# A chunked scan with a gated feed-forward layer: six steps in another order, last rows copied by whole banks, and one output matmul for both parts of a weight

## The chip, the cores and the metric

The kernel runs on 1 core of one Trainium2 chip. The metric is the time of one execution on the device in microseconds (us), and a kernel's time is the median of its runs. "Profile" and "trace" mean the records that the hardware profiler made of one execution. The engines are named as the profile names them: PE is TensorE (PEld its weight loads), DVE VectorE, ACT ScalarE, POOL GpSimd, SP SyncE.

## The reference, cut to what matters

Four batches of eight heads and 768 positions go through a scan with decay, in chunks. The result, 3072 rows of 256, goes through a gated layer with 1536 inner columns.

```python
for c in range(S // chunk):                    # the scan, per batch and head
    L = exp(cum[:, None] - cum[None, :]) * causal
    y_intra = ((C_c @ B_c.T) * L) @ x_c
    y_inter = (C_c @ state) * exp(cum)
    y[c] = y_intra + y_inter
    state = exp(sum(la)) * state + (B_c * decay_from_j).T @ x_c
x = y, as rows of 256
gate = 1 / (1 + exp(-(x @ w_gate)))            # 3072 x 1536
out  = (gate * (x @ w_val)) @ w_out            # 3072 x 256
```

## The kernel before, in words

**Tiles.** The 768 positions are six chunks of 128, and a chunk has the rows of all four batches, 512 columns. `w_gate` and `w_val` are twelve blocks each of 128 inner columns. Where precision needs it, a matrix is kept as a high and a low part, and a product is three matmuls: high by high, high by low, low by high.

**Stages.** First come chunk 0 and the preparation of the weights. Then, for each chunk, twelve pairs of gate and value products (`gate`, `value`), 128x512 each: ACT takes the sigmoid of the gate's bank, DVE multiplies the value's bank by it (L1206), ACT or DVE casts the result to the high part of h (L1210), POOL or DVE subtracts for the low part (L1212). The scan of later chunks runs between them: small matmuls in blocks (`block`), and on DVE the decays' scan (L575), six small steps a pair of batches for the state (`after`: mask L677, update L755 twice, mask, update twice), the weighing of a block (`weights`, L778) and a transposition (`turn`, L840). `proj` multiplies h by `w_out`.

**The last two chunks** (T2 = 4 and T1 = 5) go through gate and value together, as a 2x2 product by seven instead of eight blocks: for each of twelve groups (`group`, even ones gate, odd ones value) seven products of three matmuls each on combined inputs (L1369). `corner` puts four results together from three banks: ACT copies a bank to a tile (L1402), DVE adds another bank to it (L1404), then comes the sigmoid (L1407) for a gate group, or a multiplication with the gate's result (L1411) for a value group; the corner "12" is one bank alone (L1391, L1395). `h_parts` makes the two parts of h: a cast on ACT (L1421), a subtraction on DVE or POOL (L1423). `out_of` multiplies them by `w_out` and adds up in four banks (L1445): each step takes two of the four batches, and for each batch three matmuls of 256 columns: high h by both weight parts, low h by the high part. The names 11, 22, 12, 21 give inner block and chunk; 11 and 21 go to chunk T1. `stored_rows` copies one batch at a time, 256 columns, from a bank to a tile (L1459) and stores it, 128 KB (L1461): eight copies and eight stores.

**Order.** Nothing is scheduled at run time. The text `ORDER` names each step with its engine; a step issues its instructions in that place of its engine's queue, and the engines work their queues in order. Three banks of `ps_mm` are handed round among gate products, value products and `proj`; a product's step waits until the bank from three tiles before was read. In the groups each bank has its own turn: a value group's corner 12 must be read by DVE before the next gate group's third product can start in that bank.

Of the kernel before, what the change touches and what calls it, by code (L numbers as in the profile page):

```python
# [65 lines left out]
pool.decays3_0 dve.after2_0 pe.value1_2 sp.a3_2 act.gate1_2 dve.after2_0 dve.after2_0 pool.part14  # L66
dve.weights2_2 sp.a3_3 pe.gate1_3 dve.value1_2 pool.before2_2 act.part15 sp.b3_2 dve.after2_0 act.value1_2
pe.value1_3 sp.x3_0 dve.after2_0 act.gate1_3 sp.p3_0 pool.value1_2 dve.weights2_2 pe.gate1_4 dve.value1_3
sp.a4_0 pool.part15 act.value1_3 pe.value1_4 sp.a4_1 dve.turn3_0 act.gate1_4 act.part16 pe.gate1_5
pool.value1_3 sp.t3_2 act.turn3_0 dve.value1_4 dve.value1_4 pool.part16 pe.value1_5 act.gate1_5 pool.value1_4  # L70
act.part17 pe.block2 dve.value1_5 pool.part17 act.value1_5 pool.value1_5 pe.gate1_6 dve.result2_0 act.inner2_2
sp.x3_2 dve.decays3_1 act.result2_0 pe.value1_6 act.gate1_6 pool.result2_0 dve.after2_2 dve.weights3_0
pe.gate1_7 pool.decays3_1 dve.result2_0 sp.b4_0 pool.before3_0 dve.value1_6 act.result2_0 sp.a4_2
pool.result2_0 pe.value1_7 dve.weights3_0 act.value1_6 dve.after2_2 act.gate1_7 sp.a4_3 pool.value1_6
pe.gate1_8 dve.value1_7 act.value1_7 dve.after2_2 pe.value1_8 dve.after2_2 act.gate1_8 pool.value1_7
pe.gate1_9 dve.value1_8 dve.after2_2 act.value1_8 dve.after2_2 pe.value1_9 act.gate1_9 pool.value1_8 sp.p3_2
pe.gate1_10 dve.value1_9 dve.turn3_2 act.value1_9 pe.value1_10 act.gate1_10 pool.value1_9 sp.t4_0 act.turn3_2
pe.gate1_11 dve.value1_10 dve.decays3_2 act.value1_10 pe.value1_11 act.gate1_11 pool.value1_10 pe.block3
dve.value1_11 pool.decays3_2 act.value1_11 dve.decays3_3 pe.proj1_0 pool.value1_11 dve.result2_2 act.inner3_0
# [10 lines left out]
dve.weights4_2 act.gate2_2 sp.t5_0 pool.result3_2 dve.weights4_2 pool.decays5_0 pe.gate2_3 dve.result3_2  # L90
pool.decays5_1 dve.value2_2 act.result3_2 pool.result3_2 pe.value2_3 act.value2_2 dve.after4_0 act.gate2_3
pool.value2_2 pe.gate2_4 dve.value2_3 sp.p4_2 dve.after4_0 act.value2_3 dve.after4_0 pe.value2_4 dve.after4_0
sp.x5_0 act.gate2_4 pool.value2_3 pe.gate2_5 dve.value2_4 pool.before4_2 act.value2_4 pe.value2_5 dve.after4_0
# [33 lines left out]
pe.group2 act.part0_12 dve.part0_21 pe.group2 dve.corner2_11 pool.part0_12 pe.group2 act.corner2_11 pe.out0_11  # L127
act.corner2_21 pe.group2 dve.corner2_21 pe.out0_22 act.corner2_21 dve.corner2_22 pe.out0_22 act.corner2_22
pe.group2 pe.group3 act.corner2_12 dve.s8 pe.group3 act.corner3_11 dve.s8 pe.out0_12 act.corner3_22 pe.group3
act.s8 pe.group3 dve.corner3_11 pool.s8 pe.group3 act.corner3_21 pe.out0_12 dve.corner3_11 pe.group3  # L130
dve.corner3_21 act.part1_11 pe.out0_21 dve.corner3_22 pool.corner3_21 pe.out0_21 pe.group3 dve.corner3_22
act.part1_21 pe.group4 dve.part1_11 act.part1_22 pe.group4 dve.part1_22 act.corner4_11 pe.out1_11
dve.corner3_12 pool.part1_21 act.corner4_22 pe.group4 act.part1_12 dve.part1_12 pe.group4 pe.group4
dve.corner4_11 pool.s9 act.corner4_21 pe.out1_11 act.corner4_11 dve.corner4_21 pe.group4 dve.s9 act.corner4_21
pe.out1_22 dve.corner4_22 act.s9 pe.out1_22 act.corner4_22 dve.s9 pe.group4 pe.group5 act.corner4_12 dve.s10
pe.group5 act.corner5_11 dve.s10 pe.out1_12 act.corner5_22 pe.group5 act.s10 pe.group5 dve.corner5_11 pool.s10
pe.group5 act.corner5_21 pe.out1_12 dve.corner5_11 pe.group5 dve.corner5_21 act.part2_11 pe.out1_21
dve.corner5_22 pool.corner5_21 pe.out1_21 pe.group5 dve.corner5_22 act.part2_21 pe.group6 dve.part2_11
act.part2_22 pe.group6 dve.part2_22 act.corner6_11 pe.out2_11 dve.corner5_12 pool.part2_21 act.corner6_22
pe.group6 act.part2_12 dve.part2_12 pe.group6 pe.group6 dve.corner6_11 pool.s11 act.corner6_21 pe.out2_11  # L140
act.corner6_11 dve.corner6_21 pe.group6 dve.s11 act.corner6_21 pe.out2_22 dve.corner6_22 act.s11 pe.out2_22
act.corner6_22 dve.s11 pe.group6 pe.group7 act.corner6_12 pe.group7 act.corner7_11 pe.out2_12 act.corner7_22
pe.group7 pe.group7 dve.corner7_11 pe.group7 act.corner7_21 dve.corner7_11 pe.out2_12 dve.corner7_21
act.part3_11 pe.group7 dve.corner7_21 pe.out2_21 dve.corner7_22 pool.part3_11 act.part3_21 pe.out2_21
pe.group7 dve.corner7_22 pe.group8 dve.corner7_12 pool.part3_21 act.part3_22 pe.group8 act.corner8_11
pe.out3_11 dve.part3_22 act.part3_12 pe.group8 act.corner8_22 dve.part3_12 pe.group8 dve.corner8_11 pe.group8
act.corner8_11 pe.out3_11 act.corner8_21 pe.group8 dve.corner8_21 pe.out3_22 act.corner8_21 dve.corner8_22
pe.out3_22 act.corner8_22 pe.group8 pe.group9 act.corner8_12 pe.group9 act.corner9_11 pe.out3_12
act.corner9_22 pe.group9 pe.group9 dve.corner9_11 pe.group9 act.corner9_21 dve.corner9_11 pe.out3_12
# [50 lines left out]
def tile_ssd_then_gated_ffn(  # L200
# [11 lines left out]
    nc = tc.nc  # L212
# [1250 lines left out]
    def joined_tasks(t):  # L1463
# [14 lines left out]
        for k in (T2, T1):  # L1478
            for at in range(2):
                task(t + 110.0 + (k == T1), f"rows{k}_{at}", stored_rows(k, at))  # L1480
# [374 lines left out]
```

## Time and profile before

| | |
|---|---|
| runs of the kernel | 355.91, 357.05, 356.99 us |
| median | 356.99 us |
| the profiled execution | 356.6 us |
| its span, first to last instruction | 354.7 us |
| PE busy | 345.0 us, 97% of the span, 3328 matmuls |
| PE weight loads | 277.1 us, 78% |
| DVE busy | 230.5 us, 65% |
| ACT busy | 175.1 us, 49% |
| POOL busy | 170.3 us, 48% |
| moved by DMA | 27.43 MB, mean 77 GB/s |
| mean granted TensorE clock | 0.998 of full speed |

A timeline row has the start and the duration in us, the engine, the line, the operation, its tiles as out<-in, the shape and the count of instructions merged in it; in brackets stands how long the engine was idle just before and what ended that. Rows of matmuls overlap, since a matmul's duration has its way through the array in it: starts tell the pace. PE busy is no measure of how well PE is used.

### The profile page before, as it was taken

The numbers are of one execution on the slowest core, as the hardware profiler recorded it, in microseconds if no ns is written. First come the engines' busy times: TensorE is split into PE (matmuls) and PEld (weight loads), VectorE is DVE, ScalarE is ACT, GpSimd is POOL, SyncE is SP. The second block draws the span as 40 slices with busy tenths as digits, with TensorE's granted clock in tenths as the row PEclk, the third lists the DMA queues.
The fourth block names the chain that finished last, engine by engine and source line by source line (L and its number), as shares of the span: only waits on it lengthen the run. The fifth ranks groups of instructions, "written<-read, shape, count | busy, mean of one in ns | idle before, by whom it ended". The sixth has DMA issues, their size and how long they took to land.

```text
span 354.7 us, 8271 instructions
## 1 busy us (share of the span) xinstructions
PE 345.0 (97%) x3328; PEld 277.1 (78%) x3328; DVE 230.5 (65%) x405; ACT 175.1 (49%) x330; POOL 170.3 (48%) x179
## 2 busy tenths in 40 slices
PE   8989999999999999999999999999999999999995
PEld 3568477787778888888888788888888888888884
DVE  6778668787697677684653246358765778574462
ACT  2575874425946541244551235543546565654533
POOL 6435676646769664235646746864101615032100
PEclk9999999999999999999999999999999999999999
DMA  7999884335655635634300011000002000000003
GB/s 160 221 262 216 248 258 135 110 79 95 134 130 126 129 70 113 105 77 90 63 16 4 2 37 24 0 0 2 1 0 61 1 0 2 0 0 2 0 2 118
DMA packets 87467, 27.43 MB, mean 77 GB/s; under 512 B 75718, under 2 KB 80262, under 8 KB 87430
## 3 DMA queue, kind: packets, MB, share of 16 engines
q1 hardware_dynamic: 82838, 26.13, 31.3%
q10 hardware_dynamic: 4592, 0.79, 1.2%
q8 instruction: 26, 0.43, 0.5%
q14 instruction: 11, 0.09, 0.1%
HBM read 23.46 MB, written 3.44 MB: 76 GB/s over the span
## 4 chain that ended last, share of the span: by engine, by line
PE 64%; DVE 4%; ACT 1%; POOL 1%; issue 1%; ACTq 0%; DVEq 0%; POOLq 0%
PE po L1506 14%; PE pg L1245 13%; PE pv L1245 12%; PE acc L1445 6%; PE gva L1369 6%; PE gvb L1369 5%; PE gvd L1369 4%; PE banks L785 1%; DVE c L1404 1%; DVE h L1423 1%; PE banks L769 1%; ACT h L1421 1%; PE banks L815 1%; POOL c L1411 1%; DVE c L1411 1%
## 5 line engine op out<-in xcount | busy, mean ns | idle before, releaser
L1212 POOL TENSOR_TENSOR h<-g,h 128x512 fp32r<-128x512 f32 x35 | 47.4, 1356 | 36.5 <-ACT h L1210 35.2
L1245 PE MATMUL pg<-xh,w 128*128 128x512 f32 x168 | 59.4, 394 | 0.9 <-DVE g L1206 0.9
L1245 PE MATMUL pv<-xh,w 128*128 128x512 f32 x168 | 58.9, 391 | 0.1
L1506 PE MATMUL po<-h,w 128*128 128x512 f32 x216 | 51.3, 392 | 0.0
L1206 DVE TENSOR_TENSOR g<-pv,g 128x512 f32<-128x512 f32 x36 | 24.8, 689 | 35.2 <-PE pv L1245 34.7
L1506 PEld LDWEIGHTS po<-h,w 128*128 128x128 f32 x216 | 40.2, 188 | 8.6
L1445 PEld LDWEIGHTS acc<-w,h 128*128 128x128 f32 x288 | 38.8, 190 | 3.2 <-DVE h L1423 0.4
L1445 PE MATMUL acc<-w,h 128*128 128x256 f32 x288 | 39.9, 283 | 0.2 <-DVE h L1423 0.2
L1210 ACT CAST h<-g 128x512 fp32r<-128x512 f32 x34 | 21.1, 621 | 36.5 <-DVE g L1206 36.4
L1245 PEld LDWEIGHTS pg<-xh,w 128*128 128x128 f32 x168 | 31.5, 188 | 9.1 <-DVE g L1206 1.3
L1245 PEld LDWEIGHTS pv<-xh,w 128*128 128x128 f32 x168 | 31.5, 188 | 7.2 <-POOL w L497 0.5
L1245 PE MATMUL pg<-xl,w 128*128 128x512 f32 x84 | 32.7, 390 | 0.0
L1245 PE MATMUL pv<-xl,w 128*128 128x512 f32 x84 | 32.7, 389 | 0.0
L1185 ACT ACTIVATE g<-pg 128x512 f32<-128x512 f32 x44 | 26.3, 599 | 12.5 <-PE pg L1245 12.3
L497 POOL TENSOR_TENSOR w<-wr,w 128x512 fp32r<-128x512 f32 x18 | 25.8, 1437 | 7.5 <-ACT w L495 7.1
L575 DVE TENSOR_TENSOR_SCAN ab<-ab,delta 128x512 f32<-128x512 f32 x20 | 27.1, 1374 | 2.3 <-DMA ab<-a_z 2.3
L1423 POOL TENSOR_TENSOR h<-c,h 128x512 fp32r<-128x512 f32 x7 | 11.4, 1646 | 35.5 <-ACT h L1421 35.5
L478 POOL TENSOR_TENSOR wr<-wr 128x512 int32<-128x512 int32 x18 | 20.0, 1115 | 12.7 <-ACT wr L476 7.9
L1545 PE MATMUL po<-wr,h 128*128 128x256 f32 x96 | 23.4, 394 | 0.2 <-DVE h L1202 0.2
L1421 ACT CAST h<-c 128x512 fp32r<-128x512 f32 x24 | 14.7, 622 | 16.4 <-DVE c L1411 13.0
L1404 DVE TENSOR_TENSOR c<-gva,c 128x512 f32<-128x512 f32 x12 | 8.3, 691 | 20.8 <-PE gva L1369 20.8
L1545 PEld LDWEIGHTS po<-wr,h 128*128 128x128 f32 x96 | 17.6, 188 | 4.4 <-DVE h L1202 0.7
(191 smaller groups left out, 664.4 us busy)
## 6 DMA issues: line engine op xcount, KB each, us to landing
ab<-a_z SPq DMA_DIRECT2D x40, 128.0 KB
wr<-in_moe_w_gate_dram SPq DMA_DIRECT2D x6, 512.0 KB
wr<-in_moe_w_val_dram SPq DMA_DIRECT2D x6, 512.0 KB
wr<-in_moe_w_out_dram SPq DMA_DIRECT2D x6, 512.0 KB
xn<-in_x_dram SPq DMA_DIRECT2D x10, 256.0 KB
out_dram<-o SPq DMA_DIRECT2D x48, 32.0 KB
bn<-in_B_dram SPq DMA_DIRECT2D x10, 128.0 KB
out_dram<-o SPq DMA_DIRECT2D x9, 128.0 KB
```

The lines of the kernel that those rows point to most:

```text
L478: nc.gpsimd.tensor_tensor(out=lw.bitcast(I32), in0=hw.bitcast(I32), in1=lw.bitcast(I32), op=ALU.add)
L497: engines[eng].tensor_tensor(out=lo, in0=lw, in1=hi.bitcast(F32), op=ALU.subtract)
L575: nc.vector.tensor_tensor_scan(out=t.rearrange("p h l -> p (h l)"), data0=t.rearrange("p h l -> p (h l)"), data1=delta.rearrange("p h l -> ...
L1185: nc.scalar.activation(gs[k, f], pm, AF.Sigmoid)
L1206: nc.vector.tensor_tensor(out=g, in0=pm, in1=g, op=ALU.mult)
L1210: copies[eng](hh, g)
L1212: engines[eng].tensor_tensor(out=hl, in0=g, in1=hh.bitcast(F32), op=ALU.subtract)
L1245: nc.tensor.matmul(pm, w[:, part, kt, fs], xx[:, kt], start=(i == 0), stop=(i == 3 * NK - 1))
L1369: nc.tensor.matmul(out, one, two, start=m == 0 and n in (1, 7, 2), stop=m == 2, skip_group_check=True)
L1445: nc.tensor.matmul(acc[:, k * DM : (k + 1) * DM], one(js), w[:, two, :], start=first and m == k == 0, stop=final and m == 2, skip_group_ch ...
L1506: nc.tensor.matmul(acc, w[:, part], hs[k, f][:, of_h], start=f == starts[0] and i == 0, stop=f == starts[-1] + size - 1 and i == 2,)
L1545: nc.tensor.matmul(acc[:, :DM], hs[k, f][:, js], whole[NF + f // 2][:, f % 2], start=start, stop=stop, skip_group_check=True,)
```

## The change

Six places of the order move, as each engine's own queue sees them:

- DVE: value1_2 goes ahead of the third and fourth step of `after2_0` and of the first weighing of pair 2_2; value1_3 goes ahead of the second weighing.
- ACT: the copy of corner2_21 goes ahead of the sigmoid of corner2_11.
- DVE: corner3_12 goes ahead of the low part of h for 1_22, and corner5_12 ahead of that for 2_22.
- PE: the second half of out4_21 goes ahead of the last but one product of group 11.
- DVE and ACT: corner11_12 and the parts of h for 5_12 go ahead of corner11_21's multiplication and the parts for 5_21; the steps that copy the last rows are new.

In the last step the rows of chunk T2 and the first two batches of T1 are copied from a whole bank (512 columns) to one tile of 2 KB in each partition, and stored with one DMA of 256 KB. The other two batches of T1 (`at` = 1) have a bank each, a fourth bank of the pool `ps_gv` being added: high h is multiplied by both weight parts in one matmul of 512 columns into the two halves of the bank, low h by the high part into the left half. The last step of `out_of` puts all three into the left half, so the right half is complete one step before: ACT copies the right half (`last_rows`), and DVE adds the left one to it behind the last matmul.

The diff, cut: of the order's text only the moved steps with their neighbours in the engine's own queue, of the code the functions whose work changes.

```diff
-dve.after2_0 dve.after2_0 dve.after2_0 dve.after2_0 dve.weights2_2 dve.value1_2
-dve.after2_0 dve.after2_0 dve.weights2_2 dve.value1_3 dve.turn3_0
+dve.after2_0 dve.after2_0 dve.value1_2 dve.after2_0 dve.after2_0 dve.weights2_2
+dve.after2_0 dve.after2_0 dve.value1_3 dve.weights2_2 dve.turn3_0
...
-act.part0_21 act.part0_12 act.corner2_11 act.corner2_21 act.corner2_21
+act.part0_21 act.part0_12 act.corner2_21 act.corner2_11 act.corner2_21
...
-dve.part1_11 dve.part1_22 dve.corner3_12 dve.part1_12
+dve.part1_11 dve.corner3_12 dve.part1_22 dve.part1_12
...
-dve.part2_11 dve.part2_22 dve.corner5_12 dve.part2_12
+dve.part2_11 dve.corner5_12 dve.part2_22 dve.part2_12
...
-pe.out4_12 pe.group11 pe.out4_21 pe.group11 pe.out4_21 pe.group11 pe.out5_22
+pe.out4_12 pe.group11 pe.out4_21 pe.out4_21 pe.group11 pe.group11 pe.out5_22
...
-dve.part5_11 dve.part5_22 dve.corner11_21 dve.corner11_21 dve.corner11_12
-dve.part5_21 dve.part5_12 dve.rows5_0 dve.rows5_1
+dve.part5_11 dve.part5_22 dve.corner11_12 dve.corner11_21 dve.part5_12
+dve.corner11_21 dve.part5_21 dve.rows4_1 dve.rows5_2 dve.rows5_3
-act.part5_22 act.part5_21 act.part5_12 act.rows4_0 act.rows4_1 act.rows4_0
-act.rows4_1 act.rows5_0 act.rows5_0 act.rows5_0 act.rows5_1 act.rows5_1
+act.part5_22 act.part5_12 act.part5_21 act.rows5_2 act.rows5_3 act.rows4_0
+act.rows5_0 act.rows5_0 act.rows5_3
-sp.rows4_0 sp.rows4_1 sp.rows4_0 sp.rows4_1 sp.rows5_1
+sp.rows4_0 sp.rows4_1 sp.rows5_2
...
         if ("acc", block, at) not in bank:
             if (block, at) == (T1, 1):
                 bank["acc", block, at] = ps_y.tile([P, 512], F32, tag="py", name="acc")
+            elif (block, at) == (T1, 2):
+                bank["acc", block, at] = bank["pool"].tile([P, 512], F32, tag="e", name="acce")
...
             for k in range(2):
                 js = slice((2 * at + k) * P, (2 * at + k + 1) * P)
+                alone = block == T1 and at == 1
+                acc = acc_of(block, at + k if alone else at)
+                mine = acc[:, :DM] if alone else acc[:, k * DM : (k + 1) * DM]
+                if alone and not final:
+                    nc.tensor.matmul(
+                        acc, hh(js), w.rearrange("p i m -> p (i m)"), start=first, stop=False, skip_group_check=True
+                    )
+                    nc.tensor.matmul(mine, hl(js), w[:, 0, :], start=False, stop=False, skip_group_check=True)
+                    continue
                 for m, (one, two) in enumerate(((hh, 0), (hh, 1), (hl, 0))):
                     nc.tensor.matmul(
-                        acc[:, k * DM : (k + 1) * DM], one(js), w[:, two, :], start=first and m == k == 0,
-                        stop=final and m == 2, skip_group_check=True,
+                        mine, one(js), w[:, two, :], start=first and m == 0 and (k == 0 or alone), stop=final and m == 2,
+                        skip_group_check=True,
                     )
...
     def stored_rows(k, at):
...
-        for n in range(2):
-            b = 2 * at + n
-            eng = yield step(("act", "dve"), (ACT_HALF, DVE_HALF), [("o7", j, last, at)])
...
-            half = acc_of(k, at)[:, n * DM : (n + 1) * DM]
-            copies[eng](o.rearrange("p (m t) -> p t m", t=2), half.rearrange("p (t m) -> p t m", t=2))
...
+        eng = yield step(("act", "dve"), (ACT_MM, DVE_MM), [("o7", NF // 2 - 1, "21" if k == T1 else "12", at)])
+        o = wk.tile([P, 2, DM], F32, tag="m", name=f"o{k}_{at}", bufs=4)
+        copies[eng](o.rearrange(by_tk, t=2), acc_of(k, at).rearrange(by_k, k=2, t=2))
+        eng = yield step(("sp", "act"), (0.45, 0.36))
+        (nc.scalar if eng == "act" else nc.sync).dma_start(rows_of(k, 2 * at, 2), o)
+
+    def last_rows(b):
+
+        yield step("act", ACT_HALF, [("o7", NF // 2 - 1, "11", 1)], [("low", b)])
+        acc = acc_of(T1, b - 1).rearrange(by_k, k=2, t=2)
+        o = wk.tile([P, 1, DM], F32, tag="o", name=f"o{T1}_{b}", bufs=2)
+        by_t = o.rearrange(by_tk, t=2)
+        nc.scalar.copy(by_t, acc[:, 1:])
+        yield step("dve", DVE_HALF, [("o7", NF // 2 - 1, "21", 1)])
+        nc.vector.tensor_tensor(out=by_t, in0=acc[:, :1], in1=by_t, op=ALU.add)
+        eng = yield step(("sp", "act"), (0.45, 0.36))
+        (nc.scalar if eng == "act" else nc.sync).dma_start(rows_of(T1, b, 1), o)
```

## Rows read from the trace of the kernel before

**Rows 1.** The chain that ended last, from the page: its shares of the span by engine.

```profile
PE 64%; DVE 4%; ACT 1%; POOL 1%; issue 1%; ACTq 0%; DVEq 0%; POOLq 0%
```

**Rows 2.** Waits of PE from 100 us on: us in total, times, longest us.

```profile
PE pg L1245 <- DVE g L1206: 0.9, 1, 0.9
PE gvb L1369 <- DVE c L1395: 0.6, 2, 0.4
```

**Rows 3.** Timeline of PE at the step from value1_3 to gate1_4.

```profile
101.64 0.39 PE L1245 MATMUL pv<-xh,w 128*128 128x512 f32 x1
102.91 0.50 PE L1245 MATMUL pg<-xh,w 128*128 128x512 f32 x1 [0.88 <-DVE g L1206]
```

**Rows 4.** Timeline of DVE, 99 to 105 us.

```profile
99.61 1.85 DVE L755 SCALAR_TENSOR_TENSOR sm<-sq,pp,ml 128x64 f32<-128x64 f32 x2
...
102.18 0.68 DVE L1206 TENSOR_TENSOR g<-pv,g 128x512 f32<-128x512 f32 x1
102.78 0.47 DVE L755 SCALAR_TENSOR_TENSOR sn<-sm,pp,mr 128x64 f32<-128x64 f32 x2
...
104.09 0.69 DVE L1206 TENSOR_TENSOR g<-pv,g 128x512 f32<-128x512 f32 x1 [0.25 <-issue]
```

**Rows 5.** Timeline of POOL, 99 to 105 us.

```profile
101.33 0.73 POOL L857 TENSOR_TENSOR cd<-bct,pp 128x256 f32<-128x256 f32 x1
103.58 1.29 POOL L1212 TENSOR_TENSOR h<-g,h 128x512 fp32r<-128x512 f32 x1 [1.51 <-ACT h L1210]
104.84 1.56 POOL L497 TENSOR_TENSOR w<-wr,w 128x512 fp32r<-128x512 f32 x1
```

**Rows 6.** Timeline of POOL and DVE, 86.4 to 88.3 us.

```profile
86.45 1.30 POOL L497 TENSOR_TENSOR w<-wr,w 128x512 fp32r<-128x512 f32 x1 [0.35 <-ACT w L495]
86.51 1.70 DVE L607 SCALAR_TENSOR_TENSOR sn<-sm,pp,mr 128x64 f32<-128x64 f32 x2
...
87.71 0.41 POOL L585 TENSOR_TENSOR bd<-bn,ab 128x128 f32<-128x128 f32 x1
```

**Rows 7.** Timeline in the last two chunks, group 2 and then group 4.

```profile
269.19 0.87 PE L1445 MATMUL acc<-w,h 128*128 128x256 f32 x6
...
269.50 0.57 ACT L1402 COPY c<-gva 128x512 f32<-128x512 f32 x1
...
270.11 0.53 PEld L1369 LDWEIGHTS gva<-xt,s 128*128 128x128 f32 x3 [0.27 <-ACT c L1402]
...
280.31 2.38 DVE L1423 TENSOR_TENSOR h<-c,h 128x512 fp32r<-128x512 f32 x2
...
282.10 0.87 PE L1445 MATMUL acc<-w,h 128*128 128x256 f32 x6
...
283.35 0.96 PE L1369 MATMUL gvb<-x,w 128*128 128x512 f32 x3 [0.37 <-DVE c L1395]
...
284.15 0.85 PE L1369 MATMUL gva<-xt,s 128*128 128x512 f32 x3
```

**Rows 8.** The chain in order of time, 283 to 292 us: start, us on the chain, what.

```profile
285.68 0.71 PE acc L1445 x6
286.39 0.69 PE gva L1369 x3
```

**Rows 9.** Timeline of the tail, from 342 us on.

```profile
342.38 1.46 DVE L1423 TENSOR_TENSOR h<-c,h 128x512 fp32r<-128x512 f32 x2
...
345.64 1.23 ACT L1421 CAST h<-c 128x512 fp32r<-128x512 f32 x2 [2.53 <-DVE c L1411]
...
348.43 0.39 ACT L1459 COPY o<-acc 128x256 f32<-128x256 f32 x1 [1.56 <-PE acc L1445]
348.84 2.54 SPq L1461 DMA_DIRECT2D out_dram<-o  x5
```

**Rows 10.** DMA from 345 to 355 us, in 40 slices, and what was moved.

```profile
GB/s 0 0 0 0 0 0 0 0 0 0 0 0 0 0 0 0 0 0 33 344 148 78 348 185 352 344 336 348 340 328 348 332 316 17 0 0 0 0 0 0
DMA packets 1152, 1.05 MB, mean 105 GB/s; under 512 B 128, under 2 KB 1152, under 8 KB 1152
```

More of the change, by code (lines that the diff above doesn't have):

```diff
@@ L65 @@
 pool.value1_1 dve.before2_0 dve.decays3_0 act.part14 pe.gate1_2 act.inner2_0 sp.a3_1 dve.after2_0
[L66 to L79, printed above, removed]
@@ L90 @@
[L90 to L93, printed above, removed]
+pool.decays3_0 dve.after2_0 pe.value1_2 sp.a3_2 act.gate1_2 dve.value1_2 dve.after2_0 dve.after2_0 pool.part14
@@ new lines @@
+dve.weights2_2 sp.a3_3 pe.gate1_3 pool.before2_2 act.part15 sp.b3_2 dve.after2_0 act.value1_2 pe.value1_3
+sp.x3_0 dve.after2_0 act.gate1_3 sp.p3_0 pool.value1_2 dve.value1_3 dve.weights2_2 pe.gate1_4 sp.a4_0
+pool.part15 act.value1_3 pe.value1_4 sp.a4_1 dve.turn3_0 act.gate1_4 act.part16 pe.gate1_5 pool.value1_3
+sp.t3_2 act.turn3_0 dve.value1_4 dve.value1_4 pool.part16 pe.value1_5 act.gate1_5 pool.value1_4 act.part17
+pe.block2 dve.value1_5 pool.part17 act.value1_5 pool.value1_5 pe.gate1_6 dve.result2_0 act.inner2_2 sp.x3_2
@@ L131 @@
[L131 to L135, printed above, removed]
@@ L162 @@
+dve.corner11_22 pe.out4_21 pe.group11 dve.part5_11 act.part5_22 dve.part5_22 pe.group11 dve.corner11_12
+dve.corner11_21 act.part5_12 pe.out5_22 pe.out5_22 dve.part5_12 dve.corner11_21 pe.out5_11 act.part5_21
+pe.out5_11 act.rows5_2 act.rows5_3 dve.part5_21 pe.out5_12 pe.out5_12 pe.out5_21 pe.out5_21 act.rows4_0
+sp.rows4_0 dve.rows4_1 sp.rows4_1 act.rows5_0 act.rows5_0 dve.rows5_2 sp.rows5_2 dve.rows5_3 act.rows5_3
 """
@@ L1363, in group @@
                 scan_banks.close()
-                ps_gv = ctx.enter_context(tc.tile_pool(name="ps_gv", bufs=1, space=PSUM))
+                ps_gv = bank["pool"] = ctx.enter_context(tc.tile_pool(name="ps_gv", bufs=1, space=PSUM))
                 bank["gv"] = [ps_gv.tile([P, 512], F32, tag=n, name=f"gv{n}") for n in "adb"]
@@ L1477, in joined_tasks @@
                 task(t + 15.0 * j + (15.0, 18.0, 21.0, 24.0)[m], f"out{j}_{n}", out_of(j, n))
-        for k in (T2, T1):
-            for at in range(2):
-                task(t + 110.0 + (k == T1), f"rows{k}_{at}", stored_rows(k, at))
+        for k, at in ((T2, 0), (T2, 1), (T1, 0)):
+            task(t + 110.0 + (k == T1), f"rows{k}_{at}", stored_rows(k, at))
+        for b in range(2, NB):
+            task(t + 112.0, f"rows{T1}_{b}", last_rows(b))
     gs = {}
```

104 lines of the change are left out of this document (57 added, 47 removed).

## The prediction

> **What bounds the kernel now.** I read the chain that ended last first: 64% of it is TensorE [rows 1]. So a change pays where TensorE stands still, where it has less to issue, or behind its last product. The table of waits then says where it stands still after 100 us [rows 2], and the timeline gives each wait its place.
>
> The first is among the gate and value products of chunk 1. The last matmul of value1_3 starts at 101.64, gate1_4 only at 102.91 [rows 3]: 1.27 us from start to start where three such matmuls take 0.69 [rows 8], 0.23 each, so 1.04 us are lost. Gate1_4 waits for a bank that VectorE empties with the multiplication at 102.18 [rows 4].
>
> The others are in the last two chunks, where seven products make a group. There six output matmuls take 0.71 and a product 0.69 [rows 8]. Output matmuls that start at 282.10 should let the next product start at 282.81; it starts at 283.35, and the one behind it 0.80 later instead of 0.69 [rows 7]: 0.65 lost. Its twin, one pair of groups later, has what is left of the 0.6 us of idle time [rows 2], 0.2; in the first one 0.37 of idle time went with 0.65 of loss, so the twin lost about 0.2 and the same 0.28, 0.50. At 270.11 ScalarE is late: 269.19 and 0.71 make 269.90, so 0.21, and 0.11 of start-up again, 0.33 lost [rows 7].
>
> Last I read the tail [rows 9] and the slices of its DMA [rows 10], each of 0.25 us. The first store is issued at 348.84; bytes begin to move at the end of the slice that ends at 349.75, 0.89 later. The flow stalls twice (slices of 148 and 78, then of 185 GB/s), and runs from 351.0 to 353.25 without a gap at 316 to 352 GB/s. 1.05 MB at some 340 GB/s is 3.1 us. The span ends 1.4 us behind the last byte (354.7 less 353.25). So the end is set by the start of the first store and by the gaps in the flow, less by the last matmul.
>
> The profiled execution took 356.6 us: its span of 354.7 and 1.9 around it. The median of the runs is 356.99 and one had 355.91. The sum is made against 356.6.
>
> **Part 1: two value products (VectorE) ahead of steps of the state.** value1_2 now stands behind one of the two small state updates instead of both, the mask step and the weighing. The updates begin at 99.61 [rows 4], so it runs at 99.9 instead of 102.18. Gate1_4 then finds its bank free at 101.87. What is late next is value1_3: gate1_5 needs its bank twelve matmuls later, at 104.6, and ahead of it on VectorE still stand the mask step, the weighing (these end at 102.2, as before) and the second pair of state updates. That pair is the trap. ScalarE's cast follows the earlier value1_2, so GpSimd's subtraction for that tile, at 103.58 after 1.51 us of idle time, moves to 102.06, right behind the operation of 0.73 at 101.33; its next one, of 1.56, then follows without a pause [rows 5]. The updates take 0.47 at 102.78 with GpSimd idle, but 1.85 at 99.61 [rows 4]; at 86.51 a pair took 1.70, while GpSimd worked from 86.45 and again from 87.71 [rows 6]: each update waits out one GpSimd operation. So with the pair due at 102.2, the first is held to about 103.4, the second, behind the operation of 1.56, to about 104.9, and value1_3 ends at 105.6, not at 104.78. Gate1_5 starts at 105.6, where it stood at 105.76 before (102.91, twelve matmuls, 0.11). Of 1.04 I keep 0.15. The ends are 0 (the whole stop moves) and 1.04 (no hold). I take 0.15, nearest to rows 6, the same kind of pair beside a busy GpSimd. Behind value1_3 on VectorE wait a weighing and a transposition, wanted by the block of small matmuls after value1_5; they shift by 0.8, and have 2.7 us until then. The table has no other wait of TensorE until the last two chunks [rows 2], so what is won here stays won.
>
> By the Trainium skill, "SBUF — State Buffer", section "Who interferes with whom", a VectorE instruction with two SBUF inputs contends with GpSimd's reads, and one with a single SBUF input does not; rows 4 to 6 agree, and by it the pair is held. Without it the sum would be 0.9 us lower, which is the first rival.
>
> **Part 2: corner2_21's copy ahead of corner2_11's sigmoid on ScalarE.** The copy runs at 269.50 [rows 7], behind a sigmoid that it doesn't depend on. Ahead of it, it ends before 269.90, and 0.33 is won. The sigmoid comes some 0.5 later; its result is first multiplied a group later. Ends 0.2 (start-up stays) and 0.33.
>
> **Part 3: corner3_12 and corner5_12 ahead of a subtraction on VectorE.** Two subtractions took 2.38 at 280.31 [rows 7], where two take 1.46 in rows 9; corner3_12 stood behind them. Between them it starts at 281.0 and ends at 281.7; TensorE wants its bank at 282.81. It reads a bank and one tile, like the multiplication at 104.09, which took 0.69 beside GpSimd's operation from 103.58 [rows 4, 5]. The subtraction behind it was held before, and is held no longer now. Gains 0.65 and 0.50; ends half of each and the whole.
>
> **Part 4: six output matmuls ahead of a product that waits, near the end (TensorE), and the last group's corners in a new order.** This covers short stops, but the tail hangs on the first store, whose corners are VectorE's and ScalarE's to make: 0 by itself. What it could be worth is in part 6's upper end.
>
> **Part 5: h by both weight parts.** For two batches of the last chunk, in 11 of 12 steps, two matmuls of 256 columns on the same h become one of 512. A 256 takes 0.71/6 = 0.118, a 512 0.69/3 = 0.230 or a little less [rows 8]: 0.006 to 0.011 for each of 22 pairs, 0.13 to 0.24; I take 0.2, as pairs in the tail don't count. Ends 0 and 0.24. The bank that is added was another tile's before and is idle by then.
>
> By the Trainium skill, "TensorE: Matmul & The Clock Gate", section "Back-to-back issue gap", 256 columns take 262 cycles and 512 take 518; as an estimate from that page a pair would win 0.0025 us, and the sum would come out 0.15 higher.
>
> **Part 6: the stores.** Eight half copies and eight stores of 128 KB become three whole copies, four half operations, three stores of 256 KB and two of 128. From the end of the two subtractions at 343.84 [rows 9] I lay out the new order: corner11_12 and corner11_21's add (0.61 and 0.69), ScalarE's cast beside the second, a subtraction (0.69), corner11_21's multiplication (0.61): 346.45. ScalarE casts (0.62, a pair takes 1.23 in rows 9), then does two half copies that need no late matmul (0.39 alone, 0.3 each in a row), then the first whole copy, 0.57 as in rows 7: about 348.15. So the first store goes out 0.7 earlier than at 348.84. The other whole copies and the adds follow the last matmuls with stores at 348.75, 349.4, 349.6 and 350.0, each before the flow that begins at 349.05 has worked off the one before. So the gaps close, and the flow ends 3.1 us after 349.05, at 352.15 against 353.25. Gain 1.1. Ends 0.4 (the gaps alone) and 1.5 (part 4 brings the last corners 0.4 forward as well).
>
> **The sum.** 0.15 + 0.33 + 0.65 + 0.50 + 0.2 + 1.1 = 2.93: 353.7 us. I say 353.6, since part 1 has more room to win than to lose.
>
> **The rivals.** First, the second update isn't held: part 1 gives 1.04, 352.7. For it: GpSimd's operation has only 0.1 us on the update (102.06 against 102.2). Against it: rows 6. Chance 0.24. Second, the tail gives nothing: the two half copies stand ahead of the first whole copy on ScalarE, the first store is no earlier than now, and the flow starts late and has all of 1.05 MB before it: 354.7. For it: in rows 9 the first copy waits for matmuls and nothing else. Against it: the gaps in rows 10. Chance 0.14. Third, the moves don't do what they say: behind each removed wait the next dependency of the same bank comes as late, as in part 1, and under 1.07 us is left, some 356. For it: a bank is handed round between three engines. Against it: VectorE ends corner3_12 a full 1.1 us ahead of need. Chance 0.07. Fourth, slower: the holds of part 1 spread to the block after value1_5. It is due at 108.3 (105.6 and twelve matmuls); if it is late by over 4.0 us (2.93 and 1.07), the end lies above 357.7. That takes three more holds of 1.3 to 1.6 in VectorE's queue. For it: GpSimd's work there has no pause after its move. Against it: what stands behind value1_3 reads banks or one tile. Chance 0.04. The forecast has 0.51.
>
> **The numbers.** 0.3% is 1.07 us, about what a measurement here can tell from no change. Faster by more: 0.51 + 0.24 + 0.14 = 0.89; within: 0.07; slower: 0.04. The range runs from all upper ends (1.04, 0.33, 1.15, 0.24, 1.5: 352.3, less 0.2 for the spread of runs) to the second rival and the 0.4 by which the median lies above the profiled run: 352.1 to 355.1.
>
> **What would show it.** Right: no wait of 0.9 at gate1_4 but one of about 0.9 at gate1_5, with the second pair of updates at 2.5 us or more; no wait on L1395; products 0.69 apart around 270, 282 and 299; the flow of stores in slices of 330 to 350 GB/s without a gap. Wrong: no wait at either gate (first rival), a flow that starts as late behind the last group as now (second), or a stop of TensorE after the block (fourth).

## The result, and the profile after

The changed kernel took 352.18 us (median of 5 runs, 351.94 to 352.82) against 356.99 us of the kernel before: a ratio of 0.9878, interval 0.9861 to 0.9896. The forecast was 353.6 us, range 352.1 to 355.1. The profiled execution took 352.14 us with a span of 350.4, so it is compared with 356.6 and 354.7 of before: 4.3 us of span.

The waits of PE in the changed kernel, whole span (us in total, times, longest us):

```profile
PE warm L259 <- DVE table L264: 1.1, 1, 1.1
PE pg L1140 <- POOL wr L477: 0.7, 1, 0.7
PE pg L1140 <- ACT xw L1066: 0.5, 2, 0.3
PE pcb L657 <- DVE m L640: 0.2, 1, 0.2
```

None of them lies behind 60 us. Both rows of [rows 2] are gone, and so is a third of before, which [rows 2] leaves out and the forecast passed over (waits of PE, kernel before):

```profile
PE acc L1445 <- DVE h L1423: 0.2, 1, 0.2
```

**The gates of chunk 1.** PE at the steps value1_3 to gate1_4 and value1_4 to gate1_5, then DVE, POOL and SP around them, in the changed kernel:

```profile
100.94 0.39 PE L1244 MATMUL pv<-xh,w 128*128 128x512 f32 x1
101.16 0.39 PE L1244 MATMUL pg<-xh,w 128*128 128x512 f32 x1
...
103.66 0.39 PE L1244 MATMUL pv<-xh,w 128*128 128x512 f32 x1
103.88 0.39 PE L1244 MATMUL pg<-xh,w 128*128 128x512 f32 x1
```

```profile
99.14 0.68 DVE L1205 TENSOR_TENSOR g<-pv,g 128x512 f32<-128x512 f32 x1
...
101.44 0.95 DVE L754 SCALAR_TENSOR_TENSOR sn<-sm,pp,mr 128x64 f32<-128x64 f32 x2
102.32 0.68 DVE L1205 TENSOR_TENSOR g<-pv,g 128x512 f32<-128x512 f32 x1
...
101.48 0.83 POOL L856 TENSOR_TENSOR cd<-bct,pp 128x256 f32<-128x256 f32 x1 [0.84 <-DMA pp<-a_q]
102.27 1.29 POOL L1211 TENSOR_TENSOR h<-g,h 128x512 fp32r<-128x512 f32 x1
...
98.39 1.22 SPq L429 DMA_DIRECT2D pp<-a_q  x2
```

Both gates follow 0.22 us behind the matmul ahead of them, where gate1_4 stood 1.27 behind in [rows 3]. The second pair of state updates took 0.95 us, not the 2.5 or more that was forecast, because GpSimd's `cd` came late: GpSimd stood idle for 0.84 us until the load `pp` had landed, and its subtraction (102.27) started only when both updates had begun.

**The last two chunks.** PE at group 2 and at group 4, and DVE's corner3_12 (L1394):

```profile
267.38 0.39 PE L1449 MATMUL acc<-w,h 128*128 128x512 f32 x1
...
268.06 0.88 PE L1368 MATMUL gva<-xt,s 128*128 128x512 f32 x3
...
279.94 0.88 PE L1455 MATMUL acc<-w,h 128*128 128x256 f32 x6
280.65 0.86 PE L1368 MATMUL gvb<-x,w 128*128 128x512 f32 x3
281.35 0.85 PE L1368 MATMUL gva<-xt,s 128*128 128x512 f32 x3
```

```profile
278.18 0.68 DVE L1422 TENSOR_TENSOR h<-c,h 128x512 fp32r<-128x512 f32 x1
278.78 0.69 DVE L1394 TENSOR_TENSOR c<-gvb,c 128x512 f32<-128x512 f32 x1
279.38 1.18 DVE L1422 TENSOR_TENSOR h<-c,h 128x512 fp32r<-128x512 f32 x1
```

Six output matmuls at 279.94 take 0.71 and the product behind them 0.70; [rows 7] had 1.25 and 0.80 there. The step at 267.38, now four matmuls, takes 0.68 (to the product's start at 268.06), where [rows 7] had 0.92 from 269.19 to the weight load at 270.11.

**The tail.** PE from the last product in bank gva on, ScalarE's first copies and SP's first stores; then the flow, from 340 to 352 us in slices of 0.3 us:

```profile
335.26 0.85 PE L1368 MATMUL gva<-x,w 128*128 128x512 f32 x3
...
340.15 2.51 PE L1455 MATMUL acc<-w,h 128*128 128x256 f32 x18
...
343.21 2.68 PE L1455 MATMUL acc<-w,h 128*128 128x256 f32 x21
345.72 0.52 PE L1455 MATMUL acce<-w,h 128*128 128x256 f32 x3
```

```profile
343.83 0.40 ACT L1479 COPY o<-acce 128x256 f32<-128x256 f32 x1
344.12 0.64 ACT L1469 COPY o<-acc 128x512 f32<-128x512 f32 x1
...
344.79 1.17 SPq L1471 DMA_DIRECT2D out_dram<-o  x2
```

```profile
GB/s 0 0 0 0 55 0 0 0 0 0 0 0 0 0 0 0 0 0 14 317 331 318 341 331 355 341 338 352 341 116 0 0 0 0 0 0 0 0 0 0
```

The flow has no gap any more, as forecast, where [rows 10] have slices of 148, 78 and 185. But compare PE with the same stretch of the kernel before:

```profile
338.67 0.85 PE L1369 MATMUL gva<-x,w 128*128 128x512 f32 x3
...
340.77 0.87 PE L1445 MATMUL acc<-w,h 128*128 128x256 f32 x6
341.79 0.96 PE L1369 MATMUL gvb<-xb,s 128*128 128x512 f32 x3
...
343.99 3.43 PE L1445 MATMUL acc<-w,h 128*128 128x256 f32 x26
347.65 2.90 PE L1445 MATMUL acc<-w,h 128*128 128x256 f32 x22 [0.23 <-DVE h L1423]
```

From 340.77, six matmuls at 0.118 us would end at 341.48; the product starts 0.31 later and is followed at 0.11 over its pace. From 343.99, 26 matmuls at 0.118 would end at 347.06; the next starts at 347.65, 0.59 later, though the table of waits gave this stop 0.2. In the changed kernel only 0.2 is lost, in the 18 matmuls at 340.15. And the span ends as far behind PE's last row in both: 354.7 less 350.55 (347.65 and 2.90) is 4.15 us before, 350.4 less 346.24 is 4.16 after. That raised the main question of the experiments: is the tail's gain that of the stores, or that of these stops?

**Where to measure from.** Executions differ by up to 2 us in the first 60 us, before any edit: the first matmul `po` starts at 61.24 in the profile before and at 60.53 in the one after, and between 60.07 and 62.16 in all fourteen. So 0.7 of the 4.3 us is spread between executions; it is not the clock, which was granted in full (1.00) in both profiles until behind the last matmul. Medians carry this spread as well, and the experiments ran in several series on several chips, beside which the kernel before had medians of 355.7 to 357.4. The changed kernel ran in two of them, so a median beside its 352.18 says little below 1 us, and the readings below go by the profiles. Below, part 1 is measured from that matmul to gate1_6 (49.47 us before, 48.35 after, so 1.12 won) and the tail from the last product in bank gva to the end of the span (354.7 less 338.67, 16.0 before; 350.4 less 335.26, 15.1 after).

### The profile page after: what moved, and what is told of

It reads as the page before. It is cut to its first block, busy times and chain, and to the rows that moved or that the text cites. A ratio compares the mean times of both kernels' runs of the same rounds, so it can differ in the third digit from the quotient of the medians.

```text
span 350.4 us, 8223 instructions
## 1 busy us (share of the span) xinstructions
PE 343.4 (98%) x3306; PEld 275.9 (79%) x3306; DVE 231.2 (66%) x406; ACT 174.6 (50%) x328; POOL 170.9 (49%) x179
## 4 chain that ended last, share of the span: by engine, by line
PE 86%; DMA 2%; DVE 2%; ACT 1%; POOL 1%; SPq 1%; issue 0%; POOLq 0%; DVEq 0%; ACTq 0%
PE pg L1244 16%; PE pv L1244 16%; PE po L1529 14%; PE acc L1455 8%; PE po L1568 7%; PE gva L1368 6%; PE gvb L1368 6%; PE gvd L1368 5%; DMA wr<-in_moe_w_val_dram 2%; PE banks L784 2%; PE banks L768 1%; PE banks L814 1%; PE acce L1449 1%; POOL w L496 1%; PE acc L1449 1%; DVE wr L459 1%
## 5 line engine op out<-in xcount | busy, mean ns | idle before, releaser
L1455 PEld LDWEIGHTS acc<-w,h 128*128 128x128 f32 x219 | 29.8, 189 | 2.3
L1455 PE MATMUL acc<-w,h 128*128 128x256 f32 x219 | 30.6, 282 | 0.0
L496 POOL TENSOR_TENSOR w<-wr,w 128x512 fp32r<-128x512 f32 x18 | 26.7, 1483 | 7.7 <-ACT w L494 6.8
```

The costliest lines, as they stand in the source:

```text
L496: engines[eng].tensor_tensor(out=lo, in0=lw, in1=hi.bitcast(F32), op=ALU.subtract)
L1455: nc.tensor.matmul(mine, one(js), w[:, two, :], start=first and m == 0 and (k == 0 or alone), stop=final and m == 2, skip_group_check=True,)
```

## The experiments

Unless said otherwise the diffs are against the changed kernel, and show the steps of one engine's own queue.

### Part 1 undone

```diff
-dve.value1_2 dve.after2_0 dve.after2_0 dve.weights2_2 dve.after2_0 dve.after2_0 dve.value1_3 dve.weights2_2
+dve.after2_0 dve.after2_0 dve.weights2_2 dve.value1_2 dve.after2_0 dve.after2_0 dve.weights2_2 dve.value1_3
```

> The changed kernel with part 1 alone undone: value1_2 and value1_3 are back behind the state steps on VectorE. Theory (no hold: part 1 gave the whole stop): TensorE again stands still for about 1.0 us at gate1_4, none at gate1_5, and the time goes from 352.2 to about 353.2 (353.0 to 353.4). Rival (the forecast's hold did happen, and the gain seen at this place was luck of the run): the stop at gate1_4 comes back but the time grows by only 0.15 us, 352.3. Second rival (the stop is absorbed later, TensorE having slack at a later place): shift of about 1.0 at gate1_4 that shrinks before 260 us.

353.97 us (6 runs, 352.95 to 354.29). Behind 61 us the stop is back at gate1_4 and nowhere else: gate1_6 comes 49.46 us behind the first `po`, 1.11 more than in the changed kernel, and that shift stays to the end. The median lies above the theory's bounds; 0.74 of the 1.8 us by which this profile's span is longer came before 61 us.

### Parts 2 and 3 undone

```diff
-act.corner2_21 act.corner2_11 act.corner2_21
+act.corner2_11 act.corner2_21 act.corner2_21
...
-dve.part1_11 dve.corner3_12 dve.part1_22
+dve.part1_11 dve.part1_22 dve.corner3_12
...
-dve.part2_11 dve.corner5_12 dve.part2_22
+dve.part2_11 dve.part2_22 dve.corner5_12
```

> The changed kernel with parts 2 and 3 undone: corner2_21's copy behind corner2_11's sigmoid on ScalarE, corner3_12 and corner5_12 behind a subtraction on VectorE. Theory (each removed wait was worth its place, nothing late behind it): 0.35, 0.66 and 0.52 us lost again at the products near 268, 281 and 297 us, time 352.2 + 1.5 = 353.7 (353.4 to 354.0). Rival (the banks are handed round and the tail absorbs it, because the end hangs on the first store and its corners on VectorE and ScalarE): the steps come back near those places, but the span grows by less than 0.8 us, below 353.0.

354.82 us (10 runs, 353.71 to 355.51). Against the changed kernel the products lose 0.36 us at 269, 0.66 at 282 and 0.50 at 298, 1.5 together, and nothing is taken up behind them. One of the stops, PE of this kernel:

```profile
282.64 0.96 PE L1368 MATMUL gvb<-x,w 128*128 128x512 f32 x3 [0.40 <-DVE c L1394]
```

The span grew by 2.6, more than the 1.5 expected: 0.7 came before 61 us, and about 0.35 from gate1_5 to gate1_6, where nothing had been edited. That was the first hint of the hold.

### Parts 1 to 3 alone, on the kernel before

> The kernel before with parts 1, 2 and 3 alone, its last rows, stores and output matmuls as they were. Theory (parts add up: 1.04 + 0.33 + 0.65 + 0.50 = 2.5): 354.5 against 357.0 (354.2 to 354.8), first store about 2.5 earlier than at 348.84 of the kernel before, a gap in the flow of stores as before. Rival (the tail was worth nothing, the moves did it all and the rest is spread between runs): 352.5 or less. Second rival (the tail's own waits take up part of what the moves win): above 355.2.

354.31 us (10 runs, 353.01 to 355.85), within the theory's bounds; but the kernel before had 356.06 in this series (21 runs), so by medians the moves gave 1.75 and not 2.5. The profile has the whole: from the first `po` (61.51) to the last product in gva (336.28) it takes 274.77 us, 2.66 less than before (338.67 less 61.24). The tail is the old one: 352.3 less 336.28 is 16.0 us. So parts 4 to 6 are worth some 0.9 to 1.0, most of it in the tail.

### Part 4, PE's order alone undone

```diff
-pe.out4_21 pe.out4_21 pe.group11 pe.group11 pe.out5_22
+pe.out4_21 pe.group11 pe.out4_21 pe.group11 pe.out5_22
```

> The changed kernel with part 4's move on TensorE alone undone: the second half of out4_21 behind the last but one product of group 11. Theory (short stops near the end don't set it, the end hangs on VectorE's and ScalarE's corners and the first store): TensorE stops for 0.3 to 0.5 us at that product, and the first store and the end stay within 0.1 us: 352.2 (352.0 to 352.4). Rival (the product that waits delays the last corners, so the stores too): first store 0.4 us later, 352.6.

353.03 us (4 runs, 351.82 to 353.25). The tail takes 351.1 less 335.77, 15.3 us: 0.2 more, between the theory and the rival. The stop of 0.42 is back at the product, at 338.88, but the 0.2 lost in the 18 matmuls behind it is gone: the move trades the one for the other. The first store came 9.72 behind the gva product (345.49 less 335.77), not 9.53 (344.79 less 335.26); the end followed PE.

This profile showed something else: `cd` did not wait for `pp`, the second pair of updates took 2.72 us, and gate1_5 stopped for 1.06 us. That is the stop of the forecast, in a kernel that is the changed one up to this place. Gate1_6 comes 49.37 behind `po` (109.44 less 60.07): of part 1's 1.12 us, 0.10 is left.

### The hold, forced: the load pp ahead of the loads tn

```diff
-sp.t3_0 sp.p2_2
+sp.p2_2 sp.t3_0
```

> The changed kernel with the small load pp that GpSimd's cd needs issued ahead of the loads tn on SyncE, so cd is never late. In the profile of the changed kernel cd waited 0.84 us for that load, and gate1_5 did not stop; in u4_out4's it did not wait, the pair of updates took 2.72 us and gate1_5 stopped for 1.06. Theory (the forecast's hold is real, and whether it bites hangs on when that load lands): cd without a wait, the pair of updates 2.5 to 2.8 us, gate1_5 stopped for about 1.0, time 352.2 + 1.06 = 353.2 (353.0 to 353.5). Rival (the load is not what decides; what differed was the rest of the run): the pair below 2 us and no stop at gate1_5, 352.2.

353.72 us (5 runs, 353.07 to 355.06). POOL, DVE and PE of this kernel:

```profile
102.13 0.76 POOL L856 TENSOR_TENSOR cd<-bct,pp 128x256 f32<-128x256 f32 x1
102.83 1.31 POOL L1211 TENSOR_TENSOR h<-g,h 128x512 fp32r<-128x512 f32 x1
104.08 1.57 POOL L496 TENSOR_TENSOR w<-wr,w 128x512 fp32r<-128x512 f32 x1
```

```profile
103.00 2.73 DVE L754 SCALAR_TENSOR_TENSOR sn<-sm,pp,mr 128x64 f32<-128x64 f32 x2
105.65 0.68 DVE L1205 TENSOR_TENSOR g<-pv,g 128x512 f32<-128x512 f32 x1
```

```profile
105.20 0.39 PE L1244 MATMUL pv<-xh,w 128*128 128x512 f32 x1
106.39 0.50 PE L1244 MATMUL pg<-xh,w 128*128 128x512 f32 x1 [0.80 <-DVE g L1205]
```

Without a late `pp`, `cd`, the subtraction and the next operation run back to back, and the two updates due at 103.0 end only at 105.73, as the operation of 1.57 does (104.08 and 1.57). Gate1_5 starts 1.19 behind the matmul ahead of it instead of 0.22. Gate1_6 is 49.43 behind `po`: part 1 won 0.04. The theory holds; an earlier load costs a microsecond at this place. (1.6 of the 2.8 us of span that this profile has over the changed kernel's came before 63 us.)

Over all profiles with the changed kernel's order on VectorE at this place:

| `cd` waited for `pp`, us | pair of updates, us | gate1_6 behind `po`, us |
|---|---|---|
| 0.84 (the changed kernel) | 0.95 | 48.35 |
| 0.64 (parts 2, 3 undone) | 1.90 | 48.70 |
| 0.54 (halves) | 1.81 | 48.60 |
| 0.50 (the last group's order undone) | 1.76 | 48.34 |
| 0.35 (changed kernel again) | 1.61 | 48.20 |
| 0.29 (parts 1 to 3 alone) | 1.55 | 48.29 |
| 0.21 (part 5 undone) | 1.50 | 48.39 |
| 0 (part 4's PE order undone) | 2.72 | 49.37 |
| 0 (pp first) | 2.73 | 49.43 |

What decides is which starts first, the pair or GpSimd's subtraction behind `cd`. In the last two rows the subtraction started ahead of the pair, by 0.15 and 0.17 us (100.74 and 100.89; 102.83 and 103.00), and both updates were held: 1.22 and 1.57, 1.23 and 1.58 us. With a `cd` late by 0.21 to 0.54 the pair started first: its first update took 0.27 to 0.56, only the second was held for the whole subtraction (1.31 to 1.32), and gate1_6 came at most 0.25 later than in the changed kernel.

### The hold made harmless: value1_3 ahead of the pair

Two kernels: with the load pp ahead of tn as in the experiment before, and without.

```diff
-dve.after2_0 dve.after2_0 dve.value1_3 dve.weights2_2
+dve.value1_3 dve.after2_0 dve.after2_0 dve.weights2_2
```

> As hold_pp, but with value1_3 on VectorE ahead of the second pair of state updates, and with the load of the next pp behind them. Theory (the hold harms only through what stands behind the pair in VectorE's queue): the pair is held as in hold_pp, some 2.7 us or more, value1_3 ends near 102.1, no stop of TensorE at gate1_4 or gate1_5, 1.06 us less than hold_pp. Rival (the held pair makes something else late: the weighing, the transposition or value1_4, and so the block behind value1_5): a stop of 0.5 us or more between 105 and 115 us instead, and no more than half of the 1.06 won.

> The changed kernel with value1_3 ahead of the second pair of state updates on VectorE and the load of the next pp behind them; the load order of pp and tn as in the changed kernel. Theory: no stop at gate1_4 or gate1_5 whenever pp lands, so 0 to 1.06 us less than the changed kernel, as its own profile shows one or not, and 0.3 to 0.5 us less in the median. Rival (the hold rarely bites): the same median within 0.2 us.

With pp first: 352.70 us (4 runs, 351.99 to 353.95). DVE and PE:

```profile
102.16 0.68 DVE L1205 TENSOR_TENSOR g<-pv,g 128x512 f32<-128x512 f32 x1
102.76 2.14 DVE L754 SCALAR_TENSOR_TENSOR sn<-sm,pp,mr 128x64 f32<-128x64 f32 x2
```

```profile
104.33 0.39 PE L1244 MATMUL pv<-xh,w 128*128 128x512 f32 x1
104.56 0.39 PE L1244 MATMUL pg<-xh,w 128*128 128x512 f32 x1
```

The pair is held still, for 2.14 us, and PE does not stop: gate1_6 is 48.44 behind `po`, 0.99 less than with the hold in front of value1_3. Nothing becomes late behind the pair. So the hold does its harm through the queue alone.

Without pp first: 352.52 us (5 runs, 352.05 to 353.44), beside 352.18 of the changed kernel on the same chip. `cd` did not wait in its profile, the pair took 2.14, and there was no stop (48.40). The mechanism is as the theory says, but the median is not lower (rival): with the changed kernel's order of loads the full hold stands in one profile of the eight in the table above.

### Part 5 undone

```diff
-                    nc.tensor.matmul(
-                        acc, hh(js), w.rearrange("p i m -> p (i m)"), start=first, stop=False, skip_group_check=True
-                    )
+                    for i in range(2):
+                        nc.tensor.matmul(
+                            acc[:, i * DM : (i + 1) * DM], hh(js), w[:, i, :], start=first and i == 0, stop=False,
+                            skip_group_check=True,
+                        )
```

> The changed kernel with part 5 alone undone: each output matmul of 512 columns split into two of 256 with the same sums in the same banks. By the rows of the changed kernel a step of out_11 takes 0.69 us with the wide matmul where six narrow ones take 0.71, and a step of out_21 takes 0.71 to 0.72. Theory (0.02 us for each of 5 or 6 steps, nothing for the others): 0.1 us lost over the last 80 us, 352.3. Rival (the forecast, 0.006 to 0.011 for each of 22 pairs): 0.2 us. Second rival (the narrow ones are no slower): 0.

352.98 us (4 runs, 352.77 to 353.66). By the starts on PE, a step of out_11 takes 0.713 us with narrow matmuls and 0.690 with the wide ones, in three steps; in the other two that count, both take 0.71, since the product behind waits for ScalarE. Two steps of out_21 in a row take 1.430 and 1.421, five times. Three times 0.022 and five times 0.009 make 0.11: the theory. But the products beside these steps move by 0.01 to 0.02 as well: from the first product of group 0 in bank gva to the last one it takes 87.22 us (248.72 to 335.94) against 87.08 (248.18 to 335.26), 0.14 more, between the theory and the forecast. The median can't tell that.

### The last rows by halves

```diff
-        o = wk.tile([P, 2, DM], F32, tag="m", name=f"o{k}_{at}", bufs=4)
-        copies[eng](o.rearrange(by_tk, t=2), acc_of(k, at).rearrange(by_k, k=2, t=2))
...
+        for n in range(2):
...
+            copies[eng](o.rearrange(by_tk, t=2), acc_of(k, at).rearrange(by_k, k=2, t=2)[:, n : n + 1])
...
+            (nc.scalar if eng == "act" else nc.sync).dma_start(rows_of(k, 2 * at + n, 1), o)
```

> The changed kernel with the three whole-bank copies and stores of 256 KB taken by halves again (six copies of 256 columns, six stores of 128 KB), in the changed order. Theory (the end hangs on the start of the first store, and the flow has no gap either way): the first store goes out some 0.25 us earlier, since a half copy takes 0.39 where a whole one takes 0.64, and the span ends 0.1 to 0.25 earlier. Rival (fewer and larger stores are what closed the gaps): slices of the flow below 250 GB/s come back and the end is 0.3 us or more later.

353.48 us (4 runs, 352.68 to 354.09). The flow of this kernel (340 to 352 us), its first store, and PE's last product in gva and last row:

```profile
GB/s 0 0 0 0 0 0 0 55 0 0 0 0 0 0 0 0 0 0 0 65 331 239 243 307 239 355 338 342 335 342 331 31 0 0 0 0 0 0 0 0
```

```profile
345.06 1.82 SPq L1473 DMA_DIRECT2D out_dram<-o  x4
...
335.78 0.85 PE L1369 MATMUL gva<-x,w 128*128 128x512 f32 x3
...
346.25 0.52 PE L1456 MATMUL acce<-w,h 128*128 128x256 f32 x3
```

Theory and rival were each right in part. The first store comes 9.28 behind the gva product instead of 9.53, and slices below 250 GB/s are back, which the theory had not expected. The end comes 14.9 behind that product instead of 15.1, and 3.9 behind PE's last row instead of 4.16: 0.2 by spans given to a tenth, 0.14 by the trace's own times. PE's last row kept its place, 10.7 behind the gva product in both, so what moved the end here is the stores. Larger stores close the gaps, but start later by about what the gaps cost: in this profile copying by whole banks loses 0.1 to 0.2. The medians don't show it.

### The last group's order alone undone

```diff
-dve.corner11_12 dve.corner11_21 dve.part5_12 dve.corner11_21 dve.part5_21
+dve.corner11_21 dve.corner11_21 dve.corner11_12 dve.part5_21 dve.part5_12
...
-act.part5_12 act.part5_21
+act.part5_21 act.part5_12
```

> The changed kernel with the last group's order alone undone on VectorE and ScalarE: corner11_21's multiplication and the parts of h for 5_21 ahead of corner11_12 and the parts for 5_12; the stores stay by whole banks. Theory (TensorE's last matmul sets the end: in eleven profiles the span ends 4.39 to 4.42 us behind its start, with the old stores as with the new ones, and 4.25 to 4.26 in the two with halves): TensorE stops for about 0.5 us before out5_12's last matmuls, as in the kernel before, and the span ends 4.4 behind the last matmul, so 15.1 us behind the start of the last product in bank gva, where the changed kernel has 14.64; 352.7. Rival (the forecast: the first store's start and the whole-bank stores set the end): the stop comes, but the end is 14.64 to 14.8 behind that product.

353.74 us (6 runs, 352.79 to 354.07). The 14.64 and 15.1 of the expectation count from the gva product's last matmul; the profile gives 15.11. From the product's start, as above, it is 351.3 less 335.69, 15.6 against 15.1. PE:

```profile
335.69 0.85 PE L1368 MATMUL gva<-x,w 128*128 128x512 f32 x3
...
344.24 2.53 PE L1455 MATMUL acc<-w,h 128*128 128x256 f32 x19 [0.20 <-DVE h L1422]
346.61 0.52 PE L1455 MATMUL acce<-w,h 128*128 128x256 f32 x3
```

Then ScalarE's first whole copy and SP's first stores:

```profile
345.01 0.63 ACT L1469 COPY o<-acc 128x512 f32<-128x512 f32 x1 [0.79 <-PE acc L1455]
345.67 1.16 SPq L1471 DMA_DIRECT2D out_dram<-o  x2
```

The stop is that of the kernel before, with the same 0.2 in the table, and the end stands 4.17 behind PE's last row (351.3 less 347.13). All the stores are the changed kernel's here, so the 0.5 came with PE's stop and not with the form of the stores: in this the theory holds. That the last matmul itself sets the end is not shown. The first store waited for PE too and moved with it (9.98 behind the gva product, 345.67 less 335.69, and 5.6 ahead of the end, as in the changed kernel); in the run by halves the end moved with the stores while the last matmul kept its place.

### The changed kernel again, and the best of the parts

> The changed kernel itself once more, on the same chip as the next two, to have its time beside theirs and a second profile. Theory (what gate1_5 loses hangs on when the load pp lands, in each execution anew): a median between 352.2 and 353.2 us, the profile's stop at gate1_5 between 0 and 1.06 us, larger the less cd waits for pp (0.84 us of wait gave none, 0.64 gave 0.23, none at all gave 1.06 or 1.09). Rival (the first profile is typical): no stop, 352.2.

> v3_first with the last rows by halves as in the kernel halves. Theory: no stop at either gate, and the first store 0.22 us earlier against TensorE's products than in the changed kernel with the same 5.6 us from it to the end: 0.2 us below v3_first, 0.5 to 0.7 below the changed kernel in the median, some 352.0. Rival (slices of the flow with gaps cost as much as the earlier start wins): the same as v3_first.

The changed kernel: 352.18 us (5 runs, 351.65 to 353.23), with no stop at gate1_5 though `cd` waited only 0.35; by the theory's row (0.64 gave 0.23) there might have been one, and by the table above a wait of 0.21 was enough to avoid it; so the size of the wait alone doesn't give the size of the stop. What counts is which starts first, and here too the pair (101.17) started ahead of the subtraction (101.41). The best of the parts (value1_3 first, last rows by halves): 352.67 us (6 runs, 351.93 to 354.09). Its profile has no stop at either gate, and ends 15.0 us behind the gva product (350.8 less 335.81), but the runs don't show the 0.5 expected. No version here is measurably faster than the changed kernel. By the profiles they could add 0.1 to 0.2 us in each execution and a microsecond where both updates are held; how often that is in the changed kernel no run counts, and executions spread over 1.5 us.

## Why the prediction was right, and where it was wrong

The time was right within the range, 1.4 us too high and only 0.1 above the range's lower end; with 0.7 us of spread in the first 61 us, that it fell inside is in part luck. Term by term:

| term | forecast, us | measured, us |
|---|---|---|
| part 1 | 0.15 (0 to 1.04) | 1.12, or 0.04 to 0.10 where `cd` doesn't wait for `pp` |
| part 2 | 0.33 | 0.33; 0.36 undone |
| part 3 | 0.65 + 0.50 | 0.64 + 0.48; 0.66 + 0.50 undone |
| part 4, with the order of the last corners | 0 | 0.87, the tail's whole gain; 0.2 + 0.5 undone one at a time |
| part 5 | 0.2 | 0.14, of it 0.11 in the steps themselves |
| part 6, the stores | 1.1 | about 0; whole-bank copies -0.1 to -0.2 |
| before 61 us | not a term | 0.7, spread between executions |

**Part 1** failed in one step: that the subtraction "moves to 102.06, right behind the operation of 0.73 at 101.33". The forecast left `cd` where the profile of before had it. In the changed kernel's profile `cd` was held up by its load: the first update started at 101.44, just ahead of `cd` at 101.48, and the second waited for `cd` alone; the subtraction came at 102.27. So the first rival's time came, and nearly by its reason: it had given the subtraction a lead of only 0.1 us on the update, and the updates did slip ahead of it. Why they did, a late `cd`, neither the forecast nor the rival had. The forecast's hold is a case that occurs, in one profile of the eight, but not the common one. The mechanism itself was sized well: forced, the pair took 2.73 (forecast: due at 102.2 and over by about 104.9) and left 0.04 to 0.10 of the gain (forecast 0.15). By the Trainium skill, "SBUF — State Buffer", section "Who interferes with whom", VectorE's instructions with two SBUF inputs and GpSimd's reads get in each other's way; the forced hold agrees, with 2.73 us for a pair that takes 0.47 in [rows 4] beside an idle GpSimd.

**Parts 2 and 3** were right in place and size. Nothing was late behind a removed wait, and the time saved reached the end, as undoing them shows. One reading was wrong without harm: the subtraction behind corner3_12 was to be "held no longer", but took 1.18 us at 279.38, where the one ahead of it took 0.68.

**Parts 4 and 6** made 1.1 together where 0.9 was measured, but the forecast put it all on the wrong one. The failing step is the layout of part 6: it times the first whole copy by VectorE's and ScalarE's work alone, and puts PE's stops at 0. [rows 9] had the sign against it: there this copy waits 1.56 us for a matmul, which the forecast used for its second rival only. In all fourteen profiles the copy starts 0.32 us behind the start of the sixth matmul of out5_12 (343.80 and 344.12 in the changed kernel, 348.11 and 348.43 before). The first store was 0.64 earlier against PE's products, near the 0.7 of the forecast (9.53 us behind the gva product instead of 10.17), but because PE's stops went. Of these, 0.42 lay at the product behind out4_21 (0.2 of it came back as short stops) and 0.66 among out5_12's first matmuls, the 0.59 above and the start-up behind it; 0.87 net is the tail's gain. The order of the corners, costed at 0, made 0.5 of it. Undone one at a time the two moves give back 0.7; no run undoes both, so where the remaining 0.2 lies is open. The row that told of the larger stop, 0.2 us on L1423, was passed over.

Of the forecast's sentence "So the end is set by the start of the first store and by the gaps in the flow, less by the last matmul" the runs refute the use made of it, not the dependence. The gaps closed, and from the first store to the end it takes 5.61 us instead of 5.86 (350.4 less 344.79, 354.7 less 348.84); but the whole-bank copy starts that store 0.25 later than half copies do (9.53 against 9.28), so the stores win about nothing. In the changed kernel ScalarE is no earlier than PE either: its half copies start at 343.56 and 343.83, and the whole one follows without idle time.

**Part 5** was counted over all 22 pairs; five steps of out_21 gained 0.009 instead of 0.02, and two steps of out_11 ended in a wait anyway; with the products beside the steps it is 0.14.

The sum of the measured terms, 1.12 + 0.33 + 1.12 + 0.87 + 0.14, is 3.6; with the 0.7 of the first 61 us it makes the 4.3 us between the two profiles. Against the forecast's 2.93, part 1 gave 1.0 more and the first 61 us 0.7 that no term stands for; the tail gave 0.2 less and part 5 0.06 less. The changed kernel had 352.18 in both of its series: 4.8 us less than the kernel before beside it in the one, 4.0 in the other.

## What to carry to other kernels

Follow the chain from the first store back to the bank that it copies: a store that waits for a matmul moves with the matmul, and then stops of TensorE, not stores, can be what the tail is made of, as here. A wait in the table is the idle time alone; compare the starts of matmuls with their pace (0.2 in the table was 0.66 us here). And when an operation on the engine that gets in the way is placed in time, look up what that operation waits for as well: whether a load landed up to 0.84 us late or in time decided over a microsecond.

## What the runs showed that was not expected

An earlier load made the kernel slower: with `pp` there in time, GpSimd works without a pause and holds VectorE's small updates for 2.73 us; with `pp` 0.84 late they take 0.95. The price of the hold thus differs from one execution to the next of kernels that are the same up to this place.

Stores of 128 KB leave slices of 239 to 243 GB/s early in the flow where the changed kernel's profile, with its first stores of 256 KB, has none below 317 between the first and the last slice; yet with the smaller ones the span ends earlier, by 0.1 to 0.2 us against the last matmul.
